# C of the first pair from unsplit float32 weights, by float32 products in two halves of the array

## The chip, the cores and the metric

One core of one Trainium2 chip runs the whole kernel. The metric is the device time of one execution in microseconds (us). Before the change it is 1462.33 us, the median of 3 runs (1460.45 to 1466.68).

## What is computed

The reference has three stages, in float32:

```python
p_packed = sm_attn(p, k, v)              # 8 batches, 8 heads, 576 keys, 32 packed rows, width 64
out = sm_attn(q, p_packed, p_packed)     # softmax attention of 576 queries over the 32 packed rows
x = out.transpose(0, 2, 1, 3).reshape(4608, 512)
g = x @ w_gate; val = x @ w_val          # 512 -> 1536
x = (g * sigmoid(g) * val) @ w_out       # 1536 -> 512
a = x @ w1; b = x @ w2                   # 512 -> 1024
out = ((a * b) @ w3) @ w_out2            # 1024 -> 1024 -> 512
```

The weights arrive as 8-byte floats and are turned into float32 on the chip by a few integer steps ("conversion" below).

## The kernel before, in words

**The front.** For each batch b and each half Q of its heads (16 units u), `p_packed` is formed, and `pa_PT` (line 544) puts its transpose into two tiles, `PTh` and `PTl`: a rounded high part (float32r) and the rest. The work of the front is placed by step numbers in a hand-written table (`task`, `run`); within it, the first weights are converted, split and stored as well.

**C instead of x @ w.** The gate and value products use that x is a softmax times `p_packed`: for a pair P of batches (4 pairs) and a slice f of 128 hidden columns (12 slices), `c_mm` (line 416) first forms C = p_packed transposed times the slice of `w_gate` and `w_val` (256 columns together), and `stage1` (line 643) multiplies the softmax weights by C. Exact float32 is kept by splitting: each factor is a high part and a low part, and three float32r products (high x high, high x low, low x high) take the place of one float32 product. So C costs 4 x 3 = 12 matmuls of 256 columns on the whole array (line 421), and the weights must be split beforehand by `w_split` (line 384): ACT copies the high part `wh`, POOL subtracts for the low part `wl`.

`c_out` (line 428) takes C out of PSUM and splits it in turn into `ch` (ACT, three copies) and `cl` (DVE, three subtractions). It takes three because the rows of the second batch stand in another order of the four blocks.

**The main loop** (line 857) goes over the 48 steps n = (P, f). In a step stand, in this order: `w_split` of step n+2, `wo_split`, `c_mm` of step n+1, `stage1` of the pair's first batch (`pg`, then `pv`: 12 matmuls of 288 columns each, line 655), the loads for later steps or, in pair 0, their conversion, half of `stage3` (`px`, 72 matmuls, line 680) where a group of three slices is complete, `stage1` of the second batch, parts of the query softmax of the next pair (`q_T`, `q_mm`; `psq`, line 207), and the other half of `stage3`. Each engine works through its own part in program order. In pair 0 (the first 12 steps) the conversions of all weights of `w_gate`, `w_val` and `w_out` are made as well: per step two of `wf` and one of `wof`, each three operations on DVE (lines 344, 351, 354) and one on ACT (line 341). Later pairs load the converted weights back from DRAM (`Wd`).

C of slices 0 and 1 of pair 0 is formed at the end of the front (steps 17.5 and 18.5 of the table), C of slices 2 to 11 in the main loop, in steps 1 to 10. C of all of pair 1 to 3 is formed in the main loop.

**Float32 products.** A few small products are made in plain float32 before the change too, in parts of the array: `q_mm` (line 198) has 8 calls with 32 weight columns each, which are placed at 4 column positions of the array. In the trace such a call stands as two instructions.

**PSUM.** Tiles of two banks go round: four in the main loop. The pool of the main loop is opened in step 0 and takes the banks of the front's pools; the first `pg` of the main loop takes those in which C of slice 1 stood.

Of the kernel before, what the change touches and what calls it, by code (L numbers as in the profile page):

```python
# [8 lines left out]
F32 = mybir.dt.float32  # L9
F32R = mybir.dt.float32r  # L10
# [13 lines left out]
SPD = 2.25  # L24
# [14 lines left out]
def packed_attention_moe_kernel(  # L39
# [24 lines left out]
    nc = tc.nc  # L64
# [13 lines left out]
    NPR = B // 2  # L78
# [4 lines left out]
    def pool(name, side, bufs=1, **kw):  # L83
        return tc.alloc_tile_pool(name=name, bufs=bufs, side=side, reuse_waits="tile", **kw)

    def sub(out, src, hi, on="dve"):
        eng = nc.vector if on == "dve" else nc.gpsimd
        eng.tensor_tensor(out=out, in0=src, in1=hi.bitcast(F32), op=ALU.subtract)  # L88
# [19 lines left out]
    wgv = pool("wgv", "right", bufs=2)  # L108
    pt_pool = pool("pt", "right")


    PTh = pt_pool.tile([128, 4, NPR, 128], F32R, name="PTh")
    PTl = pt_pool.tile([128, 4, NPR, 128], F32R, name="PTl")

    mask = const.tile([128, 2, 64], F32, name="mask")
    nc.vector.memset(mask, 0.0)
# [3 lines left out]
    vl = pool("vl", "left", bufs=2)  # L120
# [7 lines left out]
    def psum(name):  # L128
        ps_n[0] += 1
        return ps_at[ps_n[0] % len(ps_at)].tile([128, 2, 512], F32, tag="A", name=name)  # L130

    def psum1(name):
        return psB.tile([128, 512], F32, tag="B", name=name)
# [17 lines left out]
    def q_T(b, Q):  # L151
        t = q_t.pop((b, Q))
        qT = qp.tile([128, 2, S], F32, tag="qT", name=f"qT{b}_{Q}")
        for pr in range(2):
            nc.vector.transpose(out=qT[:, pr], in_=t[:, pr].rearrange("p n d -> p (n d)"))
        PT = qp.tile([128, 128], F32, tag="PT", name=f"PT{b}_{Q}")
        for e in range(2):
            cols = slice(64 * ((b + e) % 2), 64 * ((b + e) % 2) + 64)
            hi, lo = (x[:, 2 * Q + e, b // 2, cols].bitcast(F32) for x in (PTh, PTl))
            nc.vector.tensor_tensor(out=PT[:, 64 * e:64 * e + 64], in0=hi, in1=lo, op=ALU.add)  # L160
        qT_t[b, Q] = (qT, PT)

# [205 lines left out]
    W_t, wf_t, wst_t = {}, {}, {}  # L368

    def w_conv(f, gv):  # L370
        if gv == 0:
            wf_t[0, f] = wst_t[f] = vl.tile([128, 4, 2, 128], F32, tag="wf", name=f"wf0_{f}")
        t = wf_t[0, f]
        conv(f"w_{f}_{gv}", t[:, :, gv, :])

# [8 lines left out]
    def w_split(P, f):  # L384
        t = wf_t.pop((P, f))
        hi = wgv.tile([128, 4, 256], F32R, tag="wh", name=f"wh{P}_{f}")
        lo = wgv.tile([128, 4, 256], F32R, tag="wl", name=f"wl{P}_{f}")
        split(hi, lo, t.rearrange("p k g n -> p k (g n)"), sub_on="pool")
        W_t[P, f] = (hi, lo)
# [18 lines left out]
    C_t = {}  # L408

    def wo_split(P, f):  # L410
# [2 lines left out]
        split(hi, lo, wof_t.pop((P, f)), sub_on="pool")  # L413
        wo_t[P, f] = (hi, lo)

    def c_mm(P, f):
        wh, wl = W_t.pop((P, f))
        t = psum(f"pc{P}_{f}").rearrange("p a (k n) -> p (a k) n", k=2)
        for kt in range(4):
            for x, (a, w) in enumerate(((PTh, wh), (PTh, wl), (PTl, wh))):  # L420
                nc.tensor.matmul(t[:, kt], lhsT=a[:, kt, P, :], rhs=w[:, kt],  # L421
                                 start=(x == 0), stop=(x == 2))
        if C_t.get("later"):
            C_t["later"].append((P, f, t))
        else:
            c_out(P, f, t)

    def c_out(P, f, t):
        hi = cp.tile([128, 2, 2, 256], F32R, tag="ch", name=f"ch{P}_{f}")
        lo = cp.tile([128, 2, 2, 256], F32R, tag="cl", name=f"cl{P}_{f}")  # L430
        tv = t.rearrange("p (q e) n -> p e q n", e=2)
        nc.scalar.copy(hi[0:64], tv[0:64])
        for e in range(2):
            nc.scalar.copy(hi[64:128, 1 - e], tv[64:128, e])  # L434
        sub(lo[0:64], tv[0:64], hi[0:64])
        for e in range(2):
            sub(lo[64:128, 1 - e], tv[64:128, e], hi[64:128, 1 - e])
        C_t[P, f] = (hi, lo)
# [46 lines left out]
    def pa_s(u):  # L485


        kT = kT_t.pop(u)
        t = psum(f"psp{u}")
        for hq in range(4):  # L490
            for e in range(2):
                es = slice(64 * e, 64 * e + 64)
                nc.tensor.matmul(
                    t[hs[hq], e, 0:HS].rearrange("j (m p g) -> j g m p", m=3, g=3), lhsT=kT[es, 9, hs[hq]],
                    rhs=kT[es, 0:9, hs[hq]].rearrange("d (g m) p -> d g m p", g=3), start=True, stop=True, tile_position=(64 * e, 32 * hq))
        mx = pa.tile([128, 1], F32, tag="mx", name=f"mx{u}")
        nc.vector.reduce_max(mx, t[:, :, 0:HS], axis=AX.XY)
        nc.vector.tensor_scalar_mul(mx, mx, -scale)
        return t, mx
# [44 lines left out]
    def pa_PT(u):  # L544
        b, Q = divmod(u, 2)
        Pz = P_t.pop(u)
        tb = psum1(f"pPT{u}")
        t = tb[:, 0:128]
        nc.tensor.transpose(t, Pz.rearrange("p a b -> p (a b)"), ident)
        if u < 4:  # L550
            nc.tensor.transpose(tb[:, 128:256], Pd_t.pop(u).rearrange("p a b -> p (a b)"), ident)
            PTd = pa.tile([128, 128], F32, tag="PTd", name=f"PTd{u}", bufs=4)
            nc.scalar.copy(PTd, tb[:, 128:256])
            PTd_t[b, Q] = PTd
        at = [(2 * Q + e, b // 2, slice(64 * ((b + e) % 2), 64 * ((b + e) % 2) + 64)) for e in range(2)]
        for e in range(2):
            nc.scalar.copy(PTh[(slice(0, 128),) + at[e]], t[:, 64 * e:64 * e + 64])
        for e in range(2):
            sub(PTl[(slice(0, 128),) + at[e]], t[:, 64 * e:64 * e + 64], PTh[(slice(0, 128),) + at[e]])
# [12 lines left out]
    def task(s, fn, *args):  # L572
        extra.setdefault(s, []).append((fn, args))
# [8 lines left out]
    for s, (f, gv) in WS.items():  # L582
        task(s, w_conv, f, gv)
        for d in CVD:
            task(s + d, lambda: conv_rest.pop(0)())
        if gv == 1:
            task(s + STD, w_store, f)
            if f < 3:
                task(s + SPD, w_split, 0, f)
    task(WO0, wo_conv, 0)  # L590
    for d in CVD:
        task(WO0 + d, lambda: conv_rest.pop(0)())
# [12 lines left out]
    with tc.manual_schedule(engines=M0):  # L605
        for s in range(last + 1):
# [10 lines left out]
            if 0 <= s - 1 < U:  # L617
                x = pa_s(s - 1)
# [238 lines left out]
    for n, (P, f) in enumerate(steps):  # L857
        def at(i):
            return steps[n + i] if n + i < len(steps) else None

        if n > 0 and at(2) is not None:
            w_split(*at(2))
        wo_split(P, f)
        w3_task(P, f, 0)
        if n > 0 and at(1) is not None:
            c_mm(*at(1))
        if n == NPS:
            psC.release()
            psA.release()
            ps = tc.alloc_tile_pool(name="ps", bufs=4, space=bass.MemoryType.PSUM, reuse_waits="tile")  # L870
            ps_at[:] = [ps]
        stage1(2 * P, f)
        for what, nxt in (("w", at(3)), ("wo", at(1))):
            if nxt is not None:
                if nxt[0] > 0:
                    (w_load if what == "w" else wo_load)(*nxt)
                elif what == "w":
                    w_conv(nxt[1], 0)
                    w_conv(nxt[1], 1)
                    w_store(nxt[1])  # L880
                else:
                    wo_conv(nxt[1])
                    wo_store(nxt[1])
        w3_task(P, f, 1)
        if pend is not None:
            stage3(*pend, 0)
        w3_task(P, f, 2)
        stage1(2 * P + 1, f)
        i = n - NF
        if 0 <= i < len(w12_list):  # L890
            w12_conv(i)
        if P + 1 < NPR:
            q_tasks(2 * P + 2, 0, f)
            q_tasks(2 * P + 3, 5, f)
        if pend is not None:
            stage3(*pend, 1)
            pend = None
        C_t.pop((P, f))
        if f % GF == GF - 1:
            pend = (P, f // GF)  # L900
        if P == NPR - 1:
            if f == 0:
                aA.release()
                qp.release()
                wp = pool("wp", "left", bufs=2)
            w3_task(P, f, 3)
            if f == 9:
                assert w3_at[0] > len(w3_list)
                wp.release()
                vc.release()  # L910
                xp = pool("xp", "left", bufs=2)
                x2_prep(0, 0)
            if f == 10:
                x2_prep(0, 1)
                x2_prep(0, 2)
            if f == 11:
                x2_prep(0, 3)
                load_w12(0)
                ws_sums(0)
                for k in range(7):  # L920
                    ws_block(0, k)
# [169 lines left out]
```

## Time and profile before

| | |
|---|---|
| median of 3 runs | 1462.33 us |
| the profiled execution, its own time | 1462.87 us |
| its span (first to last instruction) | 1461.1 us |
| mean granted TensorE clock | 0.979 |
| PE busy | 95% of the span |
| DVE / ACT / POOL busy | 56% / 46% / 33% |

How to read it: PE is TensorE's matmuls, PEld its weight loads, DVE VectorE, ACT ScalarE, POOL GpSimd. "pc<-wh,PTh" means that the tile `pc` is written from the tiles `wh` and `PTh`. A share over the whole span mixes three stages: the front (to about 122 us), the main loop of 48 steps (to about 890 us), and a last stage of dense products. The change touches the front and the first quarter of the main loop only.

### The profile page before, as it was taken

The page shows a single profiled execution, that of the slowest core. Times are in us where ns is not written, and L with a number is a line of the kernel's source. Part 1 is how long each engine was busy: PE and PEld are TensorE (multiplying, and loading weights), DVE is VectorE, ACT ScalarE, POOL GpSimd, SP SyncE. Part 2 cuts the span into 40 slices and gives each one's busy share as a digit, 9 for nine tenths or more (in the row PEclk, how much of TensorE's full clock was granted, in tenths as well). Part 3 has the DMA queues.
Part 4 walks back from the last instruction along what each step waited for, and adds up shares of the span by engine and source line. Part 5 has one row for each costly group of instructions (what it writes and reads, how often), then busy time and mean ns, then how long its engine had stood idle before and what let it go on. Part 6 is the DMA issues. An engine that isn't in the chain of part 4 may idle for free.

```text
span 1461.1 us, 25415 instructions
## 1 busy us (share of the span) xinstructions
PE 1392.7 (95%) x9912; PEld 1308.5 (90%) x9912; DVE 816.9 (56%) x1220; ACT 667.0 (46%) x1117; POOL 486.4 (33%) x353
## 2 busy tenths in 40 slices
PE   6677989999999999999999999999999999999999
PEld 5467879998999999999999899989989999899997
DVE  3468899967877447566446737962333423334130
ACT  4576564546745356455553514643323323233231
POOL 0345344445443445435433312631202112021120
PEclk9788899999999999999999999999999999999999
DMA  9985565666553333114333324983736638366351
GB/s 277 245 225 174 145 174 161 187 198 184 140 163 72 108 90 82 52 51 166 109 132 121 123 68 142 322 291 118 255 111 203 194 123 252 108 208 189 126 170 44
DMA packets 175255, 230.25 MB, mean 158 GB/s; under 512 B 69408, under 2 KB 102176, under 8 KB 175136
## 3 DMA queue, kind: packets, MB, share of 16 engines
q1 hardware_dynamic: 175136, 228.64, 51.0%
q8 instruction: 78, 1.28, 0.3%
q14 instruction: 41, 0.34, 0.1%
HBM read 179.04 MB, written 49.55 MB: 156 GB/s over the span
## 4 chain that ended last, share of the span: by engine, by line
PE 72%; DVE 4%; ACT 2%; DMA 1%; issue 1%; POOL 0%; SPq 0%; DVEq 0%; ACTq 0%
PE px L680 15%; PE pA L964 14%; PE po L1028 13%; PE pB L964 7%; PE pg L655 6%; PE pv L655 6%; PE pC L964 3%; PE pc L421 3%; DVE cl L88 1%; DMA raw_w<-in_moe_w_dram 1%; DMA w12d<-w12t 1%; DVE u L662 1%; PE psq L207 1%; DVE acc L690 0%; DVE w12t L354 0%
## 5 line engine op out<-in xcount | busy, mean ns | idle before, releaser
L88 POOL TENSOR_TENSOR ul<-u,uh 128x576 fp32r<-128x576 f32 x96 | 145.5, 1520 | 224.2 <-ACT uh L92 224.1
L984 POOL TENSOR_TENSOR c<-s,s 128x384 f32<-128x384 f32 x48 | 48.8, 1017 | 376.7 <-ACT s L979 376.5
L680 PE MATMUL px<-uh,woh 128*128 128x288 f32 x768 | 166.1, 298 | 7.3 <-DVE cl L88 4.7
L680 PE MATMUL px<-ul,woh 128*128 128x288 f32 x768 | 165.4, 297 | 1.3 <-POOL ul L88 1.3
L680 PE MATMUL px<-uh,wol 128*128 128x288 f32 x768 | 165.5, 297 | 0.0
L88 POOL TENSOR_TENSOR wl<-wf,wh 128x1024 fp32r<-128x1024 f32 x48 | 117.8, 2453 | 135.0 <-ACT wh L92 115.4
L979 ACT COPY s<-pA 128x384 f32<-128x384 f32 x144 | 69.2, 481 | 181.7 <-PE pA L964 181.7
L88 DVE TENSOR_TENSOR cl<-pc,ch 64x1024 fp32r<-64x1024 f32 x144 | 120.6, 864 | 54.0 <-ACT ch L434 53.2
L680 PEld LDWEIGHTS px<-uh,woh 128*128 128x128 f32 x768 | 124.6, 190 | 9.8 <-DVE cl L88 5.1
L680 PEld LDWEIGHTS px<-ul,woh 128*128 128x128 f32 x768 | 124.4, 190 | 1.5 <-POOL ul L88 1.5
L680 PEld LDWEIGHTS px<-uh,wol 128*128 128x128 f32 x768 | 124.9, 190 | 0.0
L1028 PE MATMUL po<-wo_hi,abl 128*128 128x512 f32 x288 | 112.2, 389 | 0.0
L1028 PE MATMUL po<-wo_lo,abh 128*128 128x512 f32 x288 | 112.1, 389 | 0.0
L1028 PE MATMUL po<-wo_hi,abh 128*128 128x512 f32 x288 | 112.0, 389 | 0.0
L88 DVE TENSOR_TENSOR abl<-ab,abh 128x768 fp32r<-128x768 f32 x48 | 48.7, 1014 | 106.0 <-ACT abh L92 105.9
L92 ACT CAST uh<-u 128x576 fp32r<-128x576 f32 x96 | 64.7, 674 | 93.7 <-DVE u L662 93.4
L690 DVE TENSOR_TENSOR acc<-acc,px 128x576 f32<-128x576 f32 x96 | 70.9, 746 | 62.7 <-PE px L680 62.5
L662 DVE TENSOR_TENSOR u<-u,pv 128x576 f32<-128x576 f32 x96 | 72.1, 752 | 47.9 <-PE pv L655 42.5
L655 PE MATMUL pv<-aTh,ch 128*128 128x288 f32 x384 | 83.9, 300 | 7.8 <-ACT u L660 7.5
L88 POOL TENSOR_TENSOR wol<-wof,woh 128x512 fp32r<-128x512 f32 x48 | 65.5, 1378 | 74.6 <-ACT woh L92 65.9
L660 ACT ACTIVATE u<-pg 128x576 f32<-128x576 f32 x96 | 62.6, 652 | 60.6 <-PE pg L655 57.8
L655 PE MATMUL pg<-aTh,ch 128*128 128x288 f32 x384 | 83.9, 300 | 5.2 <-DVE cl L88 3.1
(358 smaller groups left out, 3627.2 us busy)
## 6 DMA issues: line engine op xcount, KB each, us to landing
ws<-wsd SPq DMA_DIRECT2D x245, 256.0 KB, 3.0
wf<-Wd SPq DMA_DIRECT2D x36, 512.0 KB, 3.4
raw_w<-in_moe_w_dram SPq DMA_DIRECT2D x32, 512.0 KB, 4.7
wsd<-ws SPq DMA_DIRECT2D x49, 256.0 KB, 3.0
raw_wo<-in_moe_w_out_dram SPq DMA_DIRECT2D x20, 512.0 KB, 4.2
km<-in_k_dram SPq DMA_DIRECT2D x16, 576.0 KB, 8.0
vm<-in_v_dram SPq DMA_DIRECT2D x16, 576.0 KB, 8.6
wof<-wod SPq DMA_DIRECT2D x36, 256.0 KB, 2.9
```

Source lines behind the costliest of these rows:

```text
L88: eng.tensor_tensor(out=out, in0=src, in1=hi.bitcast(F32), op=ALU.subtract)
L92: nc.scalar.copy(hi, src)
L421: nc.tensor.matmul(t[:, kt], lhsT=a[:, kt, P, :], rhs=w[:, kt], start=(x == 0), stop=(x == 2))
L655: nc.tensor.matmul(t[:, hf, 0:HS], lhsT=w[:, b % 2, Q, cols], rhs=x[:, Q, hf, :], start=first, stop=last,)
L660: nc.scalar.activation(u, t[:, :, 0:HS], AF.Silu)
L662: nc.vector.tensor_tensor(out=u, in0=u, in1=t[:, :, 0:HS], op=ALU.mult)
L680: nc.tensor.matmul(t[:, hf, 0:HS], lhsT=w[:, 128 * d:128 * d + 128], rhs=x[:, hf, :], start=first, stop=last,)
L690: nc.vector.tensor_tensor(out=o, in0=o, in1=t[:, :, 0:HS], op=ALU.add)
L964: nc.tensor.matmul(bk[n], lhsT=w[:, hl, 128 * d:128 * d + 128], rhs=r[:, d], start=(first and d == 0 and i == 0), stop=(d == 1 and i == 2) ...
L979: nc.scalar.copy(o, t)
L984: on.tensor_tensor(out=r, in0=o, in1=t, op=op)
L1028: nc.tensor.matmul(t, lhsT=a[:, j, cols], rhs=w[:, f], start=first, stop=last)
```

## The change

C of pair 0 is no longer formed from split factors. `pa_PT` writes the transposed `p_packed` of units 0 to 3 once, in float32, into a new tile `PT0`, and neither `PTh` nor `PTl` for them (these two lose their first pair). `c_first` forms C of pair 0 with 16 calls, each with all 128 rows, 64 weight columns and 256 moving columns in float32, alternately in the lower and the upper 64 columns of the array, and writes them already in the order that `stage1` wants. So `c_out` needs one copy and one subtraction for pair 0. `w_split` is not called for pair 0 any more, neither in the front (slices 0 to 2) nor in the loop. The converted weights of pair 0 stand in the buffers that held `wh` and `wl`, in turn, instead of those of `wf`.

```diff
+    PT0 = pt_pool.tile([128, 4, 2, 64], F32, name="PT0")
...
     def w_conv(f, gv):
         if gv == 0:
-            wf_t[0, f] = wst_t[f] = vl.tile([128, 4, 2, 128], F32, tag="wf", name=f"wf0_{f}")
+            wf_t[0, f] = wst_t[f] = wgv.tile([128, 4, 2, 128], F32, tag=("wh", "wl")[f % 2], name=f"wf0_{f}")
...
+    def c_first(f):
+        w = wf_t.pop((0, f))
+        t = psum(f"pc0_{f}").rearrange("p b (q n) -> p b q n", q=2)
+        for b in range(2):
+            for Q in range(2):
+                for e in (b, 1 - b):
+                    at = 64 * (e ^ b)
+                    nc.tensor.matmul(
+                        t[at:at + 64, b, Q], lhsT=PT0[:, 2 * Q + e, b],
+                        rhs=w[:, 2 * Q + e].rearrange("p g n -> p (g n)"),
+                        start=True, stop=True, tile_position=(0, at))
+        return t
+
     def c_mm(P, f):
+        if P == 0:
+            t = c_first(f)
+            if C_t.get("later"):
+                return C_t["later"].append((P, f, t))
+            return c_out(P, f, t)
...
     def c_out(P, f, t):
...
+        if P == 0:
+            nc.scalar.copy(hi, t)
+            sub(lo, t, hi)
+            C_t[P, f] = (hi, lo)
+            return
...
             PTd_t[b, Q] = PTd
+            nc.scalar.copy(PT0[:, 2 * Q:2 * Q + 2, b], t.rearrange("p (e j) -> p e j", e=2))
+            return
...
-            if f < 3:
-                task(s + SPD, w_split, 0, f)
...
-        if n > 0 and at(2) is not None:
+        if at(2) is not None and at(2)[0] > 0:
             w_split(*at(2))
```

## Rows read from the trace of the kernel before

**Rows 1.** The page, part 1: busy us, share of the span, instructions.

```profile
PE 1392.7 (95%) x9912; PEld 1308.5 (90%) x9912; DVE 816.9 (56%) x1220; ACT 667.0 (46%) x1117; POOL 486.4 (33%) x353
```

**Rows 2.** Stretches: length, busy PE, PEld, DVE, ACT, POOL; clock, DMA share, GB/s.

```profile
130.00:185.00 55.00, 50.30 (x360) 47.25 (x360) 49.12 (x57) 30.52 (x46) 23.49 (x14) 0.91 0.53 154
185.00:237.00 52.00, 44.39 (x326) 42.75 (x325) 51.74 (x66) 28.66 (x44) 22.18 (x13) 1.00 0.63 174
237.00:285.00 48.00, 45.60 (x357) 43.46 (x356) 45.34 (x65) 26.98 (x39) 20.88 (x12) 1.00 0.58 182
285.00:305.00 20.00, 18.89 (x143) 18.33 (x142) 18.98 (x25) 13.94 (x23) 13.04 (x8) 1.00 0.61 174
...
378.00:421.00 43.00, 43.00 (x328) 43.00 (x328) 36.24 (x45) 25.27 (x38) 22.02 (x13) 1.00 0.61 173
```

**Rows 3.** Waits of PE from 130 to 305 us: total, times, longest.

```profile
PE pv L655 <- ACT u L660: 5.7, 3, 2.8
PE px L680 <- DVE cl L88: 4.7, 2, 2.4
PE pc L421 <- DVE cl L88: 2.8, 4, 1.5
PE px L680 <- DVE sT L214: 1.9, 1, 1.9
PE pg L655 <- DVE u L662: 0.7, 1, 0.7
```

**Rows 4.** Groups by form, whole span: what splits C and the weights.

```profile
L88 POOL TENSOR_TENSOR wl<-wf,wh 128x1024 fp32r<-128x1024 f32 x48 | 117.8, 2453 | 135.0 <-ACT wh L92 115.4 <-issue 18.4 <-POOL ul L88 1.2
...
L88 DVE TENSOR_TENSOR cl<-pc,ch 64x512 fp32r<-64x512 f32 x96 | 62.5, 691 | 0.7
...
L88 DVE TENSOR_TENSOR cl<-pc,ch 64x1024 fp32r<-64x1024 f32 x48 | 58.2, 1212 | 53.3 <-ACT ch L434 53.2
...
L434 ACT CAST ch<-pc 64x512 fp32r<-64x512 f32 x96 | 51.3, 582 | 0.6
...
L92 ACT CAST wh<-wf 128x1024 fp32r<-128x1024 f32 x48 | 50.0, 1042 | 14.7 <-DVE wf L354 11.9 <-POOL wf L357 2.8
...
L432 ACT CAST ch<-pc 64x1024 fp32r<-64x1024 f32 x48 | 48.3, 1006 | 26.2 <-PE pc L421 26.2
```

**Rows 5.** A float32 product in four column positions: timeline, and its matmuls' durations (min/median/max).

```profile
173.97 0.43 PE L655 MATMUL pv<-aTh,cl 128*128 128x288 f32 x2
...
174.33 0.64 PEld L207 LDWEIGHTS psq<-qT,PT 128*32 128x32 f32 x16 [0.17 <-ACT wf L341]
174.33 1.18 PE L207 MATMUL psq<-qT,PT 128*32 128x288 f32 x16
...
175.81 0.42 PE L680 MATMUL px<-ul,woh 128*128 128x288 f32 x2
...
L207 PE MATMUL psq<-qT,PT x192: 406/406/689, 150.6 to 616.5; 128*32 128x288 f32 x192
```

**Rows 6.** C as it is now, timeline: its first of 12 matmuls, and what follows.

```profile
185.12 0.28 PE L421 MATMUL pc<-wh,PTh 128*128 128x256 f32 x1
...
186.56 0.42 PE L655 MATMUL pg<-aTh,ch 128*128 128x288 f32 x2
```

**Rows 7.** DVE beside POOL, timeline.

```profile
142.02 2.40 POOL L88 TENSOR_TENSOR wl<-wf,wh 128x1024 fp32r<-128x1024 f32 x1 [1.71 <-ACT wh L92]
142.05 2.91 DVE L354 SCALAR_TENSOR_TENSOR wof<-raw_wo,vx_wo 128x512 int32<-128x512 int32 x1
...
258.26 0.68 DVE L354 SCALAR_TENSOR_TENSOR wof<-raw_wo,vx_wo 128x512 int32<-128x512 int32 x1
```

**Rows 8.** The end of the front: a stretch (columns as in rows 2), and timeline.

```profile
107.00:122.00 15.00, 8.54 (x130) 7.61 (x130) 9.93 (x23) 12.09 (x25) 8.01 (x6) 0.73 0.53 154
...
119.24 2.52 DVE L88 TENSOR_TENSOR cl<-pc,ch 64x1024 fp32r<-64x1024 f32 x3
121.91 0.82 PE L655 MATMUL pg<-aTh,ch 128*128 128x288 f32 x2 [3.10 <-DVE cl L88]
```

More of the change, by code (lines that the diff above doesn't have):

```diff
@@ L109, in packed_attention_moe_kernel @@
     pt_pool = pool("pt", "right")
-    PTh = pt_pool.tile([128, 4, NPR, 128], F32R, name="PTh")
-    PTl = pt_pool.tile([128, 4, NPR, 128], F32R, name="PTl")
+    PTh = pt_pool.tile([128, 4, NPR - 1, 128], F32R, name="PTh")
+    PTl = pt_pool.tile([128, 4, NPR - 1, 128], F32R, name="PTl")
+    PT0 = pt_pool.tile([128, 4, 2, 64], F32, name="PT0")
     mask = const.tile([128, 2, 64], F32, name="mask")
@@ L158, in q_T @@
             cols = slice(64 * ((b + e) % 2), 64 * ((b + e) % 2) + 64)
-            hi, lo = (x[:, 2 * Q + e, b // 2, cols].bitcast(F32) for x in (PTh, PTl))
+            hi, lo = (x[:, 2 * Q + e, b // 2 - 1, cols].bitcast(F32) for x in (PTh, PTl))
             nc.vector.tensor_tensor(out=PT[:, 64 * e:64 * e + 64], in0=hi, in1=lo, op=ALU.add)
@@ L420, in c_mm @@
             for x, (a, w) in enumerate(((PTh, wh), (PTh, wl), (PTl, wh))):
-                nc.tensor.matmul(t[:, kt], lhsT=a[:, kt, P, :], rhs=w[:, kt],
+                nc.tensor.matmul(t[:, kt], lhsT=a[:, kt, P - 1, :], rhs=w[:, kt],
                                  start=(x == 0), stop=(x == 2))
[L423 to L426, printed above, removed]
+        c_out(P, f, t)
     def c_out(P, f, t):
@@ L554, in pa_PT @@
             PTd_t[b, Q] = PTd
-        at = [(2 * Q + e, b // 2, slice(64 * ((b + e) % 2), 64 * ((b + e) % 2) + 64)) for e in range(2)]
+            nc.scalar.copy(PT0[:, 2 * Q:2 * Q + 2, b], t.rearrange("p (e j) -> p e j", e=2))
+            return
+        at = [(2 * Q + e, b // 2 - 1, slice(64 * ((b + e) % 2), 64 * ((b + e) % 2) + 64)) for e in range(2)]
         for e in range(2):
```

## The prediction, made blind

> **What bounds the kernel now.** I read the page's busy times first: PE is busy 95% of the span [rows 1], so at first sight every microsecond added to PE is paid and none taken from another engine is won. That holds for the mean, not for the stretch that changes, so I cut the loop into stretches of three steps [rows 2]. In pair 1, from 378 to 421 us, PE is busy all 43 us while DVE has 36. In pair 0 the reader should see the two change places: from 185 to 237 us DVE is busy 51.7 of 52 us and PE only 44.4. From 130 to 305 us PE's busy times add to 159.2 of 175 us, so it stands still for 15.8. The waits of PE there give the same 15.8 us (5.7 + 4.7 + 2.8 + 1.9 + 0.7) and name who is late: ACT's `u`, and DVE's `cl`, `sT` and `u` [rows 3]. In the first stretch the granted clock is 0.91 [rows 2]: 0.09 / 0.5 x 55 = 10 us at the lower level, 1.2 GHz, where PE had just stood still. Up to 2 of these lie in the waits themselves, and half of the other 8, so 4 us, is lost work. So pair 0 holds about 19.8 us (15.8 + 4) that a PE with everything ready would not need. This is all that the loop can give back.
>
> **Part 1: the products of C.** Now C is 12 matmuls, 185.12 to 186.56: 1.44 us [rows 6]. The new form is not in the trace. The nearest is `psq`: float32, all 128 rows, in column parts of the array, with 8 calls that stand as 16 instructions [rows 5]. They take 1.18 us from the first start to the last end, and each lasts 0.406 us. Were they one after the other, 16 streams would not fit, so four run side by side, in four rounds: (1.18 - 0.406) / 3 = 0.258 us per round of 288 columns. For 256 columns that is 0.229. Twice the present pitch (1.44 / 12 = 0.12 per 256 columns of float32r) would be 0.24, so a float32 instruction streams at about half the pace of a float32r one. The new C has 16 calls, 32 instructions; in two halves that is 16 rounds, 3.5 to 3.7 us. Entering and leaving the parts of the array costs too. From 173.97 to 175.81 lie the block and two pairs of ordinary matmuls, one ahead of it and one behind [rows 5]. At the pace of rows 6 a pair takes 2 x 0.12 x 288 / 256 = 0.27 us, so the block has 1.84 - 0.54 = 1.30, and less 4 x 0.25 of streaming 0.3 us are left [rows 5, 6]. I take 3.5 + 0.25 = 3.75 us, 2.3 us more than now. Ends: 3.45 without any switch (+2.0), and 16 x 0.229 + 0.31 = 3.97 (+2.5). Ten C's stand in the main loop, where nothing hides PE's work: +22.5 us (20 to 25).
>
> **Part 2: what leaves DVE, ACT and POOL in pair 0.** Per step [rows 4]: three subtractions of `cl` (1.21 + 2 x 0.69 = 2.59 us) become one over as many elements per partition as the first of them, about 1.21, so DVE loses 1.4. ACT loses two of the three copies (2 x 0.58) and `wh` (1.04): 2.2 us. POOL loses `wl`, 2.45 us. POOL's loss is DVE's gain as well: an operation of DVE that takes 0.68 us by itself took 2.91 while `wl` ran, and ended after it [rows 7]. Over the nine C's from 130 to 285 us DVE has 146.2 us of 155 [rows 2]; less 9 x 1.4 it has 134, and if half of the time of nine `wl` was DVE standing still (9 x 2.45 / 2 = 11), 123. PE has 140.3 + 9 x 2.3 = 161. So DVE would be at 76 to 83% of PE, where pair 1 has 84% and no idle PE [rows 2]. I therefore let PE become the bound again, and most of the waits go: 14 of the 15.8 us, and the 4 us of clock with the stall before it. Late next is ACT's `u`, the longest wait now [rows 3], and what the `wl` of pair 1 hold up, which POOL still makes in the last two steps. Ends: 4 us and 19.8.
>
> **Part 3: the front.** Two C's stand there, at a mean clock of 0.73 [rows 8]; they take 2.3 us more each at the full clock and 4.6 at the lower one. The main loop begins when `cl` of the second has released its PSUM banks: 119.24 + 2.52 = 121.76, `pg` at 121.91 after 3.10 us of waiting [rows 8]. Ahead of that go three `wh` (3.1 us of ACT), three `wl` (7.4 us of POOL), two thirds of `ch` and half of `cl` for two slices (DVE 2.8 us, ACT 2.3). The longer C's delay the last units' products on PE by about as much, as these queue behind them. I take -1.5 us; ends -6 (the 2.8 of DVE, one `wh`, and 2 us of clock after a busier PE) and +5 (both C's at the lower clock, 9.2, less the relief of some 4). The single copy into `PT0` instead of two copies and two subtractions for four units is off the path: these units are done long before the last.
>
> **Part 4: buffers and DMA.** The converted weights go to the four buffers of `wh` and `wl`. The conversion for step n+3 takes the buffer of slice n-1, whose C was formed in step n-2, and whose store was issued in step n-4, so neither is late; pair 1's first split takes buffers read in step 7. Same stores and loads on SP, in the same order: no cost. If that cover failed, a conversion would wait for a store to land; `c_first` comes two steps later, and a step of pair 0 lasts 17 us now (155 us for nine), so PE would see only a delay beyond that.
>
> **The sum.** 22.5 - 14 - 4 - 1.5 = +3.0 us. The profiled execution took 1462.87 us, 0.5 above the median of the runs, so I forecast 1465.5 us. A measurement of this kernel can tell about 0.5%, 7.3 us, from no change: that is 1455 to 1469.6.
>
> **Rivals.**
>
> *The stalls stay* (slower). DVE's queue in pair 0 remains the place where the step is set, because POOL's `ul` and `wol` stop DVE as `wl` did, and a longer PE step only moves the waits. For it: DVE was full for 52 us [rows 2]. Against: pair 1 runs at 84% with the same `ul`, `wol` and even `wl`. It decides from the point where less than 22.5 - 1.5 - 7.3 = 13.7 of the 19.8 us come back. With 4 coming back and nothing from the front it is 22.5 - 4 = +18.5: 1481 us. Chance 0.20.
>
> *The front and all stalls give back* (faster). 20 us for the C's, less 19.8, less 6 in the front: -6, or 1457 us; below 1455 only if the clock of the first loop steps rises as well. Chance 0.12.
>
> *The halves take turns.* If two parts of 64 columns don't run side by side, there are 32 rounds: 32 x 0.22 + 0.25 = 7.3 us, +5.9 each, +59 in the loop, less 19.8, and some +8 in the front: 1509 us. Against it stand four parts side by side in `psq`; for it, that no row shows 64 columns. Chance 0.06.
>
> *Weight loads don't hide.* In `psq` the 16 weight loads end 0.64 us after the first start, half a microsecond before the last matmul does, so they ran under the matmuls [rows 5]. If a round instead waited for its load, at 0.15 us each (between 0.64 / 16 = 0.04 and a whole round's 0.258 [rows 5], for want of a nearer row the middle), C would take 16 x 0.15 = 2.4 us more, +24 in ten steps: all stalls returned, 22.5 + 24 - 19.8 = +27, 1489 us. The Trainium skill (TensorE: Matmul & The Clock Gate, Part 3) says that loads overlap matmuls in flight only where the groups of rows differ; here every part uses all rows, so by that rule this rival would come true, and the trace of `psq`, also all rows, disagrees. Chance 0.04.
>
> **How the numbers follow.** The forecast's own case has 0.58, by its ends 1459 to 1472. A range that leaves out the halves taking turns, the dearest of the weight-load case and the outer tails of the first two rivals is 1457 to 1484. Faster by over 0.5%: half of the second rival and a trace of the forecast, 0.08. Slower: most of the first rival (0.17), the last two (0.10) and the upper end of the forecast (0.09): 0.36. Within: 0.56.
>
> **What would show it.** `pc` of pair 0 as 32 instructions in rounds of about 0.22 us, 3.75 us in all; DVE under 85% from 130 to 290 us; PE's waits there under 5 us in total; the clock at 1.00 from 130 us on; the first `pg` of the loop within 119 to 123 us; `c12`'s place, and all after it, later by 3 us or so. I am wrong if a C takes 5 us or more, if PE's waits in pair 0 stay over 10 us, or if the loop starts over 5 us from where it did.

## The result, and the profile after

The changed kernel takes 1443.53 us (median; 1441.93 to 1444.94), the kernel before 1463.14 us on the same chip (1460.45 to 1466.68). The ratio is 0.9858, with a 95% interval of 0.9839 to 0.9876. So the change wins 20 us, where the prediction had a loss of 3: the forecast, its range and its likeliest sign were all wrong. The execution profiled here took 1441.93 us (span 1440.2), against 1462.87 before.

One number in the text ahead is false. "The change" and Part 1 say that `c_first` has 16 calls. Its three loops, over b, Q and e, have two turns each: 2 x 2 x 2 = **8 calls**, or 16 instructions, half of what the forecast paid for.

First the page's busy times (columns as in [rows 1]):

```profile
PE 1393.1 (97%) x9960; PEld 1302.1 (90%) x9960; DVE 780.2 (54%) x1188; ACT 642.5 (45%) x1077; POOL 457.7 (32%) x341
```

PE's busy time is what it was (1392.7), while the span is 21 us shorter. PE does not do less; it stands still less. DVE is busy 37 us less, ACT 24.5, POOL 29. The stretches of [rows 2] show where; after:

```profile
130.00:185.00 55.00, 55.00 (x431) 49.53 (x430) 43.44 (x65) 31.09 (x47) 15.75 (x11) 1.00 0.62 176
185.00:237.00 52.00, 52.00 (x400) 48.22 (x399) 44.58 (x62) 23.79 (x37) 17.92 (x13) 1.00 0.67 195
237.00:285.00 48.00, 47.97 (x369) 45.05 (x369) 42.01 (x58) 25.81 (x37) 21.52 (x13) 1.00 0.64 170
```

PE is busy all the time, so these stretches hold more work than they did. For the same work, from the first C of the main loop to the tenth (nine C's), before and after:

```profile
130.35:285.42 155.07, 140.37 (x1038) 133.53 (x1037) 146.62 (x186) 86.41 (x127) 66.20 (x38) 0.97 0.58 169
```

```profile
127.35:265.92 138.57, 138.57 (x1073) 126.68 (x1072) 119.23 (x171) 71.37 (x103) 44.50 (x30) 1.00 0.67 189
```

PE was busy 140.4 of 155.1 us and now all of 138.6, and the granted clock went from 0.97 to 1.00. DVE fell from 146.6 to 119.2 us. The waits of PE from 119 to 310 us, where [rows 3] had five lines and 15.8 us:

```profile
PE pg L676 <- DVE cl L88: 1.4, 1, 1.4
```

That one wait is the loop's start, which was 3.1 us [rows 8]. In the main loop of pair 0 not one wait is left. What C costs PE now, in the timeline of a step in the same place as [rows 6]:

```profile
174.02 0.42 PE L701 MATMUL px<-uh,wol 128*128 128x288 f32 x2
174.37 1.95 PE L424 MATMUL pc<-wf,PT 128*64 128x256 f32 x16
176.25 0.54 PE L676 MATMUL pg<-aTh,ch 128*128 128x288 f32 x2
176.62 0.42 PE L676 MATMUL pg<-aTl,ch 128*128 128x288 f32 x2
```

From the last pair of `px` to the second pair of `pg` are 2.60 us; two ordinary pairs take 0.54, so C holds PE for **2.06 us**, 0.62 more than the 1.44 of [rows 6]. The list of the tile's instructions (count, then shortest, median and longest in ns) says how it streams:

```profile
L424 PEld LDWEIGHTS pc<-wf,PT x192: 132/137/232, 106.8 to 267.3; 128*64 128x64 f32 x192
L424 PE MATMUL pc<-wf,PT x192: 379/379/690, 106.8 to 267.5; 128*64 128x256 f32 x192
```

192 instructions for 12 C's are 16 each. The first start and the last end of a C lie 1.95 us apart; less the 0.379 of one matmul, 1.57 us for seven steps make eight rounds of two, 0.224 us apart.

On DVE, three groups from 130 to 285 us, before (busy us, mean ns):

```profile
L354 DVE SCALAR_TENSOR_TENSOR wof<-raw_wo,vx_wo 128x512 int32<-128x512 int32 x10 | 13.3, 1328 | 0.1
L88 DVE TENSOR_TENSOR cl<-pc,ch 64x512 fp32r<-64x512 f32 x18 | 11.7, 691 | 0.1
L88 DVE TENSOR_TENSOR cl<-pc,ch 64x1024 fp32r<-64x1024 f32 x9 | 10.8, 1205 | 0.9 <-ACT ch L434 0.9
...
L160 DVE TENSOR_TENSOR PT<-PTh,PTl 128x64 f32<-128x64 f32 x8 | 6.0, 769 | 0.0
```

and after:

```profile
L88 DVE TENSOR_TENSOR cl<-pc,ch 128x1024 fp32r<-128x1024 f32 x10 | 12.1, 1211 | 3.6 <-ACT ch L448 3.6
L355 DVE SCALAR_TENSOR_TENSOR wof<-raw_wo,vx_wo 128x512 int32<-128x512 int32 x10 | 8.0, 804 | 0.0
...
L161 DVE TENSOR_TENSOR PT<-PTh,PTl 128x64 f32<-128x64 f32 x8 | 1.6, 210 | 0.0
```

The subtractions of C are one pass instead of three (22.5 us for nine C's become 12.1 for ten, 10.9 for nine). So of the 27.4 us that DVE lost over the same work they are 11.6. The other two groups were not changed at all: the last step of the ten conversions of `wof` takes 0.80 us each instead of 1.33, the eight sums for `PT` 0.21 instead of 0.77, 9.7 us together. Most of the other 15.8 us was DVE standing still inside its own instructions; single groups vary from run to run, so the tests below are read by DVE's total over nine C's.

**Where the 20.9 us lie.** The first `pg` of the loop starts 2.5 us earlier (119.42 against 121.91). The second C of pair 1 is the next mark, before:

```profile
302.75 0.39 PE L421 MATMUL pc<-wh,PTh 128*128 128x256 f32 x1 [0.27 <-DVE cl L88]
```

and after:

```profile
282.42 0.39 PE L440 MATMUL pc<-wh,PTh 128*128 128x256 f32 x1
```

That is 20.3 us earlier: 17.8 were won in the loop of pair 0, although ten C's cost 6.2 more there. The stretches between the two marks, before and after:

```profile
121.91:302.75 180.84, 165.03 (x1204) 157.63 (x1205) 171.06 (x220) 103.28 (x152) 81.91 (x47) 0.96 0.59 171
```

```profile
119.42:282.42 163.00, 162.97 (x1245) 149.82 (x1245) 138.01 (x196) 85.67 (x124) 60.53 (x39) 0.99 0.67 188
```

Behind the mark the lead dips and comes back, 0.6 us more in all. From 305 to 700 us the profiled execution has one wait (3.3 us, below), the kernel before four, of 3.4 us in all. A second profiled execution of the changed kernel took 161.69 us from mark to mark, and had three waits behind it, of some 7 us in all.

### The profile page after: what moved, and what is told of

It is laid out like the page before. It is cut to its first block, busy times and chain, and to the rows that moved or that the text cites. A ratio compares the mean times of both kernels' runs of the same rounds, so it can differ in the third digit from the quotient of the medians.

```text
span 1440.2 us, 25384 instructions
## 1 busy us (share of the span) xinstructions
PE 1393.1 (97%) x9960; PEld 1302.1 (90%) x9960; DVE 780.2 (54%) x1188; ACT 642.5 (45%) x1077; POOL 457.7 (32%) x341
## 5 line engine op out<-in xcount | busy, mean ns | idle before, releaser
L88 DVE TENSOR_TENSOR cl<-pc,ch 64x512 fp32r<-64x512 f32 (+2 forms) x120 | 105.1, 900 | 55.4 <-ACT ch L455 47.6
L88 POOL TENSOR_TENSOR wl<-wf,wh 128x1024 fp32r<-128x1024 f32 x36 | 86.9, 2414 | 97.4 <-ACT wh L92 86.7
L676 PE MATMUL pg<-aTl,ch 128*128 128x288 f32 x384 | 83.3, 299 | 0.0
```

Of the source, the lines that this page charges most:

```text
L676: nc.tensor.matmul(t[:, hf, 0:HS], lhsT=w[:, b % 2, Q, cols], rhs=x[:, Q, hf, :], start=first, stop=last,)
```

## The experiments

Four theories stood. **The count**: the forecast's method held, and the eight calls that it counted too many are most of its miss. Of what freed DVE, three more: **A**, either relief would have done alone, and only both loads together bring waits back; **B**, what counts is the split of the weights on ACT and POOL; **C**, what counts is DVE's own subtractions of C. In the tests below, but for e5, the changed kernel is the base, and one thing is put back or changed; "back" is what a run is slower than its 1443.53 us.

**e1: the calls that were counted.** Each of the eight products is issued twice, so that there are 16 calls.

```diff
-                for e in (b, 1 - b):
+                for e in (b, 1 - b, b, 1 - b):
```

> The changed kernel, with each of the 8 float32 products of a C of pair 0 issued twice (the second writes the same values over the first): 16 products per C, the number that the prediction counted. Theory (PE is the bound of pair 0 after the change, and the miss is the count): a C takes 8 rounds of 0.216 us more, 3.7 instead of 2.0 us, all of it paid in the ten C's of the loop: 17 us more than the changed kernel's 1443.5, and 2 to 5 us more in the front at the lower clock: 1461 to 1466 us, where the prediction stood. Rival (DVE and ACT still set the pace of pair 0, and PE has slack there): less than 9 us more, under 1452 us, and PE's waits shrink instead.

Measured: 1465.87 us (1464.85 to 1469.26), ratio to before 1.0021 (1.0002 to 1.0040). Its timeline:

```profile
181.22 0.42 PE L701 MATMUL px<-uh,wol 128*128 128x288 f32 x2
181.58 3.67 PE L424 MATMUL pc<-wf,PT 128*64 128x256 f32 x32
185.18 0.54 PE L676 MATMUL pg<-aTh,ch 128*128 128x288 f32 x2
185.56 0.42 PE L676 MATMUL pg<-aTl,ch 128*128 128x288 f32 x2
```

By the same reading C holds PE for 4.34 - 0.54 = 3.80 us, against the 3.75 of the forecast, and the kernel takes the 1465.5 us that were forecast. The kernel that was priced blind is this one. That the two agree to 0.4 us has some luck in it: ten C's cost 23.6 us more than before, where 22.5 were forecast, and as the kernel before took 1463.69 beside it, all the rest gave back 21.4, where 19.5 were forecast. The eight extra rounds cost 3.80 - 2.06 = 1.74 us, or 0.217 each, and ten C's 17.4 of the 22.3 us between the two kernels; the front is 1.9 us later, and 2.2 us of waits stand in the loop again.

**e2: C's three copies and three subtractions back.** The products stay as changed.

```diff
-            nc.scalar.copy(hi, t)
-            sub(lo, t, hi)
+            nc.scalar.copy(hi[0:64], t[0:64])
+            for e in range(2):
+                nc.scalar.copy(hi[64:128, e], t[64:128, e])
+            sub(lo[0:64], t[0:64], hi[0:64])
+            for e in range(2):
+                sub(lo[64:128, e], t[64:128, e], hi[64:128, e])
```

> The changed kernel, with C of pair 0 taken out of PSUM in three copies and three subtractions again, as before. DVE gets 1.4 us more per C, ACT 1.2. Theory A (DVE's queue overflowed only by the sum of its own subtractions and its stops beside POOL, so that either alone fits under PE): 1 to 5 us more than the changed kernel's 1443.5, 1444 to 1449 us, with PE's waits from 119 to 285 us under 5 us. Theory B (POOL's low parts made all the stalls): no more than 1 us. Theory C (the subtractions made them): over 10 us, 1454 us or more.

Measured: 1457.99 us, ratio 0.9957 (0.9940 to 0.9975): 14.5 us back. The profiled execution is the longest of the six (1461.20). Its stretch of nine C's:

```profile
128.56:275.96 147.40, 140.20 (x1074) 126.73 (x1073) 136.06 (x189) 81.53 (x123) 44.80 (x30) 1.00 0.62 184
```

DVE is at 136.1 us, 16.8 more than in the changed kernel, though POOL has no `wl` to make for pair 0 (44.8 us, against 44.5). The two passes more per C are 11.7 of that. So here DVE is late mostly by its own work.

**e3_idle_split: the split of the weights back.** In steps 1 to 9 ACT's copy and POOL's subtraction are made as before, into buffers that nobody reads.

```diff
+    def w_idle(f):
+        hi = vl.tile([128, 4, 2, 128], F32R, tag="wf", name=f"ih{f}")
+        lo = vl.tile([128, 4, 2, 128], F32R, tag="wf", name=f"il{f}")
+        split(hi, lo, wf_t[0, f], sub_on="pool")
...
+        elif n > 0 and at(2) is not None:
+            w_idle(at(2)[1])
```

> The changed kernel, which in the loop's steps 1 to 9 also makes the split of the weights of pair 0 (ACT's copy of the high part, POOL's subtraction of the low part, at the place where it stood before), into buffers that nobody reads. Theory A (either alone fits under PE): 1 to 5 us more, 1444 to 1449 us. Theory B (POOL's low parts made the stalls): 10 us or more, from 1453 us, with single operations of DVE of 2 us and more beside POOL's and PE's waits over 10 us in pair 0. Theory C (the subtractions of C made them): no more than 1 us.

Measured: 1458.19 us, ratio 0.9942 (0.9910 to 0.9974): 14.7 back, with DVE's subtractions still in one pass. Four of its five executions lie between 1458.13 and 1459.44, one took 1447.59. DVE has 132.1 us over nine C's, 12.9 more than in the changed kernel, though no instruction was added on DVE.

**e3_idle_three: both.** The edits of the last two together.

> Both at once: the idle split of the weights of pair 0 in the loop, and C of pair 0 taken out in three copies and three subtractions. What is left of the change in the loop is the products themselves and the buffers. Theory A (the sum of both overfills DVE's queue): over 12 us more than the changed kernel's 1443.5, 1456 us or more, and more than the two single runs add up to. Theories B and C: no more than the larger of the two single runs and 2 us. If the loop's gain lay in the new buffers for the converted weights, or in the products, all three runs stay within 3 us of 1443.5.

Measured: 1463.23 us, ratio 0.9993 (0.9979 to 1.0008): 19.7 back, the time of before. The largest of its waits of PE from 117 to 305 us:

```profile
PE pc L429 <- DVE cl L88: 4.1, 3, 2.4
PE pg L685 <- DVE cl L88: 2.7, 1, 2.7
PE px L710 <- DVE cl L88: 2.0, 2, 1.1
PE px L710 <- DVE sT L215: 2.0, 1, 2.0
```

DVE has 144.5 us over nine C's. A fell twice: each load alone brings back more than two thirds of the gain, and the two together bring 19.7, less than the 29.2 of their sum. B and C each named a half. Both loads lie on the same queue, DVE's, and once it is late, more work on it costs less than the first did. The ten C's still cost 6.2 us more than before here, yet the time is that of before: beside a late DVE the longer C takes the place of waits (13.8 us in the loop, against 15.8) and of time at the lower clock, while in the changed kernel all that e1 adds is paid.

**e3_idle_pool and e3_idle_act: which half of the split.** Only POOL's subtraction, or only ACT's copy, is put back, against the changed kernel and in the same steps. POOL has no high part to read here, so it subtracts the weights from themselves. The expectations call it D that POOL alone does it, through DVE, and E that ACT's queue does.

```diff
+    def w_idle(f):
+        lo = vl.tile([128, 4, 2, 128], F32R, tag="wf", name=f"il{f}")
+        w = wf_t[0, f]
+        nc.gpsimd.tensor_tensor(out=lo, in0=w, in1=w, op=ALU.subtract)
```

```diff
+    def w_idle(f):
+        hi = vl.tile([128, 4, 2, 128], F32R, tag="wf", name=f"ih{f}")
+        nc.scalar.copy(hi, wf_t[0, f])
```

> The changed kernel with only POOL's part of the idle split: one subtraction of 1024 elements per partition in each of the loop's steps 1 to 9, into a buffer that nobody reads. Theory D (pair 0 now runs just under the edge of DVE's queue, and DVE stops while POOL subtracts, so this alone pushes it over): 8 to 14 us more than the changed kernel's 1443.5, 1451 to 1458 us, with the idle split of both engines at 1458. Theory E (it was ACT: its copy of the high part waits for the converted weights and holds up the activation behind it): under 4 us more.

> The changed kernel with only ACT's part of the idle split: one copy of 1024 elements per partition in each of the loop's steps 1 to 9, into a buffer that nobody reads. Theory E (ACT's copy waits for the converted weights and holds up the activation behind it): 8 to 14 us more than 1443.5, with PE's waits on ACT's u. Theory D (DVE beside POOL): under 4 us more.

Measured: POOL alone 1452.67 us, ratio 0.9925 (0.9902 to 0.9947), 9.1 back; ACT alone 1443.01 us, ratio 0.9870 (0.9840 to 0.9899), nothing back that its interval of some 4 us either way can show; its profiled execution has one wait of 2.2 us. How POOL does it, in the timeline of its run:

```profile
204.61 1.89 POOL L388 TENSOR_TENSOR il<-wf 128x1024 fp32r<-128x1024 f32 x1 [3.36 <-DVE wf L355]
...
205.06 1.73 DVE L345 TENSOR_SCALAR vx_wo<-raw_wo 128x512 int32<-128x512 int32 x1
```

A step of the conversion that DVE makes in 0.41 us at its shortest in this trace takes 1.73 beside POOL's subtraction and ends after it. The stretches of nine C's say the same, with POOL's subtraction and with ACT's copy:

```profile
125.45:269.86 144.41, 140.06 (x1073) 126.89 (x1072) 127.95 (x169) 70.83 (x103) 60.58 (x39) 1.00 0.64 181
```

```profile
121.93:264.32 142.39, 140.22 (x1074) 128.22 (x1073) 120.14 (x171) 79.90 (x114) 45.11 (x31) 0.99 0.66 187
```

With one instruction per step added on POOL and none on DVE, DVE has 128.0 us, 8.7 more than the 119.2 of the changed kernel; with ACT's copy it has 120.1. The Trainium skill (SBUF — State Buffer, "SBUF: two separate sides") says that DVE and GpSimd share a pair of ports by an exclusive lock, which the one that starts first holds for its whole instruction: of DVE one in a two-port mode or, against a GpSimd instruction that reads SBUF, one with two inputs in SBUF. The conversion's last step has two such inputs, and [rows 7] agree: its 2.91 us start 0.03 us behind POOL's 2.40 and end behind them. Which mode the step with one input was in, no run here shows.

ACT's copy and POOL's subtraction together cost 14.7 us where the one costs 9.1 and the other nothing, but the two tests do not add up to the third. POOL's subtraction takes 1.95 us by itself and 2.77 in the run with both, 15.6 against 22.1 us for eight; DVE stands still for 8.7 against 12.9 us, 0.56 and 0.58 for each microsecond of POOL's. So most of the difference is the length of the subtraction. What ACT adds beyond that stays open; in the run with both, the largest wait is for ACT's `u` (4.6 us), which in the run with ACT's copy alone is 2.2.

**e5: one pass of copies and subtractions in the kernel before.** The split products stay. The blocks of the second batch then stand in the wrong order: that part of the computation is changed.

```diff
+        if P == 0:
+            nc.scalar.copy(hi, t.rearrange("p (b q) n -> p b q n", b=2))
+            sub(lo, t.rearrange("p (b q) n -> p b q n", b=2), hi)
+            C_t[P, f] = (hi, lo)
+            return
```

> The kernel before, with its split products and splits of the weights, but C of pair 0 taken out in one copy and one subtraction; the blocks of the second batch then stand in another order, so this part of the result is another one. What is left of the old form beside the changed kernel: C 0.6 us shorter on PE, and the split of the weights. Theory (DVE's queue fills from two sides, and either side alone brings back most of the waits): the idle split cost 14.7 us on top of the changed kernel; with C 6 us shorter that makes 1450 to 1457 us. Rival (the new buffers or the unsplit weights matter in another way): outside 1446 to 1460.

Measured: 1455.22 us, ratio 0.9934 (0.9912 to 0.9956), against 1465.0 for the kernel before on the same chip: 9.8 us for this part alone, half of the gain, without any float32 product. DVE has 129.1 us over nine C's, against 146.6 before.

**e4: unsplit float32 on the whole array.** Four calls of 128 columns per C; C then comes in the old order, and takes three copies and subtractions as before. `PT0` is filled by two copies per unit for it.

```diff
+        t = psum(f"pc0_{f}").rearrange("p a (k n) -> p (a k) n", k=2)
+        for kt in range(4):
+            nc.tensor.matmul(t[:, kt], lhsT=PT0[:, kt, :],
+                             rhs=w[:, kt].rearrange("p g n -> p (g n)"),
+                             start=True, stop=True)
```

> The changed kernel with C of pair 0 from unsplit float32 products on the whole array: 4 products with 128 weight columns in place of 8 with 64, so C comes in the old order of blocks and needs three copies and three subtractions. No change of the array's parts: C 1.75 us instead of 2.05, 3 us less in ten steps than the run with three pieces and the halves (1458): 1453 to 1458 us. If the halves brought more than the order of the blocks (a float32 product of 128 columns streams slower than two of 64 side by side), C takes 3 us or more and the time is above 1462. If the halves are what costs, it is under 1448.

Measured: 1448.72 us, ratio 0.9904 (0.9880 to 0.9929): 5.2 back, better than expected. Its timeline:

```profile
187.15 0.43 PE L669 MATMUL pv<-aTh,cl 128*128 128x288 f32 x2
187.41 1.89 PE L421 MATMUL pc<-wf,PT 128*128 128x256 f32 x8
188.95 0.62 PE L669 MATMUL pg<-aTh,ch 128*128 128x288 f32 x2
189.41 0.43 PE L669 MATMUL pg<-aTl,ch 128*128 128x288 f32 x2
```

C holds PE for 2.26 - 0.54 = 1.72 us: eight instructions with no change of array parts, 0.34 less than in halves. So the halves cost 0.34 per C on PE, and what they buy is the order of the rows that makes one pass of copies possible. Against e2, which shares its DVE work, this kernel is 9.3 us faster. Ten C's of 0.34 are 3.4 of that; its waits in pair 0 are 8.4 us instead of 9.3, and e2's profiled execution has one more of 2.2 us near 400 us. For the remaining 2.8 the clock is at hand: from 290 to 410 us the granted clock is 0.97 in e2 and 1.00 here, 3.6 us of work at the most. That is one execution of each.

**e6: unsplit float32 halves in all four pairs.** `c_first` takes the pair as an argument, and no weight of the gate and value products is split any more. The later pairs' weights are loaded into the buffers of `wh` and `wl` too, and a copy takes the place of the sums for `PT`.

```diff
-                        t[at:at + 64, b, Q], lhsT=PT0[:, 2 * Q + e, b],
+                        t[at:at + 64, b, Q], lhsT=PT0[:, 2 * Q + e, 2 * P + b],
...
-        if at(2) is not None and at(2)[0] > 0:
-            w_split(*at(2))
```

> The unsplit products in two halves for C of all four pairs: no split of these weights anywhere, one copy and one subtraction per C everywhere, and the query products read the unsplit tile. Theory (outside pair 0 PE is the bound and the relief of the other engines is worth nothing): 36 C's at 2.05 in place of 1.44 us, 22 us more, less up to 5 us of waits in the first steps of pair 1: 1460 to 1466 us. Rival (the relief counts in all pairs): under 1450 us.

Measured: 1466.11 us, ratio 1.0016 (0.9999 to 1.0033): 22.6 slower than the change alone. In the stretch of pair 1 that [rows 2] show:

```profile
378.00:421.00 43.00, 43.00 (x334) 39.38 (x333) 21.72 (x31) 13.34 (x21) 12.37 (x9) 1.00 0.40 125
```

DVE falls to 21.7 us of 43, and nothing comes of it: PE was full there before (43.00) and is full now. At 0.62 us each, 36 more C's are 22.3 us, all of them paid. The same edit wins 20 us where DVE is the bound and loses 22 where PE is.

**e7: the wait that is left.** The changed kernel's wait at 314 us, on ACT and DVE:

```profile
312.50 0.66 ACT L342 ACTIVATE w12t<-raw_w 128x512 f32<-128x512 f32 x1 [5.79 <-DMA w12d<-w12t]
313.20 0.69 DVE L352 SCALAR_TENSOR_TENSOR vx_w<-w12t,vx_w 128x512 int32<-128x512 int32 x1 [2.40 <-ACT w12t L342]
313.92 1.65 DVE L355 SCALAR_TENSOR_TENSOR w12t<-raw_w,vx_w 128x512 int32<-128x512 int32 x1
315.60 1.38 DVE L345 TENSOR_SCALAR vx_w<-raw_w 128x512 int32<-128x512 int32 x1
316.90 0.74 DVE L711 TENSOR_TENSOR acc<-acc,px 128x576 f32<-128x576 f32 x1
```

and on PE:

```profile
317.70 0.85 PE L676 MATMUL pg<-aTh,ch 128*128 128x288 f32 x2 [3.35 <-DVE acc L711]
318.34 0.68 PE L676 MATMUL pg<-aTl,ch 128*128 128x288 f32 x2
```

DVE's sum `acc`, for which PE waits, stands behind a conversion of the later stages' weights (`w12t`) that itself waits for ACT, and ACT waits for the store of an earlier block (`w12d<-w12t`). Behind the wait PE's pairs follow each other every 0.48 us instead of every 0.27, and the granted clock from 314 to 323 us is 0.67, where it was 1.00 from 300 to 314. Two mends: these conversions three steps later, or three buffers in place of two for them (and for the other tiles that share these buffers).

```diff
-        i = n - NF
+        i = n - NF - 3
```

```diff
-        t = vl.tile([128, 512], F32, tag="vu", name=f"w12t{i}")
+        t = vl.tile([128, 512], F32, tag="vu", name=f"w12t{i}", bufs=3)
```

> The changed kernel, with the conversion of the weights of the last stage three steps later (steps 15 to 30 in place of 12 to 27), so that it does not fall in with the end of pair 0. After the change the loop has one wait of PE of 3.3 us behind DVE's sum for px at 314 us, with a lower clock behind it; ACT there waits for the store of a converted block. Theory (the gain of pair 0 is partly given back there): 2 to 5 us less than the changed kernel, 1438 to 1442 us. Rival (the wait moves on with the conversions): within 1 us of it.

> The changed kernel, with three buffers in place of two for these converted blocks, so that a conversion does not wait for the store of the block two before it. Theory: the wait of PE at 314 us goes, 2 to 5 us less than the changed kernel, 1438 to 1442 us. Rival (the store is not what is late, the loads are): within 1 us of it.

> The changed kernel itself, beside the runs of this call: 1443.5 us, within 2.

Measured, on one chip: the changed kernel again 1442.65 us, ratio 0.9843 (0.9824 to 0.9861); later conversions 1445.40, ratio 0.9864 (0.9849 to 0.9880); three buffers 1441.94, ratio 0.9835 (0.9814 to 0.9856). Neither wins: the first is 2.8 us slower than the changed kernel beside it, with none of its four executions among the other's, and the second is within 1 us, as its rival had it. With later conversions the wait for `acc` is 2.0 us; with three buffers the one at 314 us is gone, and others stand up, of up to 2.0 us. Single waits vary: `px` waits for `cl` for 2.1 us near 387 us in the first, and as long in the second execution of the changed kernel. No version that ran clearly beats the changed kernel.

## Why the prediction was wrong, step by step

**Part 1, the products of C: the step that failed.** "The new C has 16 calls, 32 instructions": it has 8 and 16. The method held. Rounds of 0.229 us per 256 columns (from `psq`) or 0.24 (twice the float32r pace) were read, 0.22 was used, and 0.217 is measured; 0.3 us were put on the change of array parts, and 2.06 - 8 x 0.217 is 0.32. With the right count the forecast's own terms give 8 x 0.22 + 0.25 = 2.0 us, +0.6 per C and +6 for ten instead of +22.5, a sum of 6 - 14 - 4 - 1.5 = -13.5, and 1449 us. So the miscount is 16.5 of the 22 us by which the forecast missed, and e1, which has the calls that were counted, takes the time that was forecast. The diff gave the number: three loops of two turns each. The trace gave a second one, since C has 4 blocks of weight rows by 2 batches, eight products of 64 columns without the split.

**Part 2, what leaves DVE.** Right in kind and too timid. For nine C's DVE was to have 123 to 134 us, and has 119.2: it lost 27.4 us, where 12.6 to 23.6 were forecast. The subtractions are 11.6 of that, against 12.6, and the rest, most of it standing still, 15.8, against 0 to 11. DVE is at 86% of PE's 138.6 us, above the 76 to 83% that were forecast for a longer PE and near the 84% that pair 1 lives with [rows 2]. From that "14 of the 15.8 us" of waits were to go; all went. That DVE gains through POOL as well, taken from [rows 7] at half of each `wl`, is confirmed by the run with POOL's subtraction alone, which gives 9 us back. ACT's relief, named beside them, shows no gain by itself.

**A wait costs more than its idle time.** In the loop 17.8 us were won. Waits of 15.8, 4 of clock, less 6.2 for C are 13.6, so 4.2 are missing from the forecast's terms even with C and the waits as measured. The clock is 1.8 of them: at the lower level, half the speed, half of the time is lost work, so a stretch loses its length times what its mean clock lacks to 1.00. With the mean clocks above, 0.96 and 0.99 (0.959 and 0.991 with a digit more), that is 7.3 us of the 180.84 before and 1.5 of the 163.00 after, 5.8 less (some tenths of it lie in the waits), where the forecast took 4, from the stretch from 130 to 185 us alone. Most of the other 2.4 stands in the trace of before, at the 1.9 us wait of [rows 3]:

```profile
157.58 0.42 PE L655 MATMUL pv<-aTh,cl 128*128 128x288 f32 x2
159.85 0.50 PE L680 MATMUL px<-uh,woh 128*128 128x288 f32 x2 [1.85 <-DVE sT L214]
160.19 0.45 PE L680 MATMUL px<-ul,woh 128*128 128x288 f32 x2
```

The two pairs are 2.27 us apart where 0.27 would do, so 2.00 are lost and 1.85 shown: the idle time is counted from the drawn end of a matmul, which lies behind the place where the next could have started. The first pair after the wait takes 0.34 until the next instead of 0.27. That is 0.2 us for each of the 11 waits, some 2.4 in all, by this one wait; it is read from rows, not tested. The runs with something put back, each in its profiled execution, from the first `pg` to the second C of pair 1 (163.00 us in the changed kernel):

| kernel | longer by, us | PE's waits there, us | more lost to the clock, us | left, us | medians: back, us |
|---|---|---|---|---|---|
| the change, with ACT's copy | 2.4 | 2.2 | 0.2 | 0.0 | 0 |
| with POOL's subtraction | 6.4 | 4.5 | 0.0 | 1.9 | 9.1 |
| with C's three passes (e2) | 12.5 | 9.3 | 2.0 | 1.2 | 14.5 |
| with the split of the weights | 14.2 | 9.4 | 3.4 | 1.4 | 14.7 |
| with both | 17.6 | 13.8 | 1.9 | 1.9 | 19.7 |

So waits and clock together are most of what the loads cost, and 1.2 to 1.9 us are left where several waits stand, roughly 0.2 each. By the medians, the loads that cost anything cost 1.4 to 2 us for each microsecond of wait that the profile shows. Each row is one execution, and loop starts differ by some 5 us between these runs, so single rows are rough.

**Part 3, the front.** The forecast was -1.5 us, with `pg` between 119 and 123; it came at 119.42, -2.5. The two C's there were overpriced by the same count. The place varies: in a second execution of the changed kernel `pg` came at 117.83, and the kernel before has one trace.

**Part 4, buffers and DMA.** From 119 to 310 us PE waits for no store and no weight buffer, and no engine for a store of `wf`, as forecast. ACT does wait there for stores of other weights (`w12t`), 15.4 us in all (7.0 before, from 119 to 330 us), and the wait of PE at 314 us that comes of them was not foreseen.

**The rivals.** *The stalls stay* was refuted: no wait is left. *The front and all stalls give back* has its mechanism confirmed, but by the false count it ended at 1457 us, and so the way that it went was given 0.08. *The halves take turns* is refuted by eight rounds, not sixteen, for 16 instructions (sixteen of 0.217 us would be 3.5 us, and a C takes 2.06). *Weight loads don't hide* is refuted too: the loads last 0.137 us, and rounds follow each other every 0.217, so nothing is left between two rounds in which two of them could stand. By one of its rules the Trainium skill (TensorE: Matmul & The Clock Gate, Part 3) lets a load overlap running matmuls only where the groups of rows differ; here every product uses all 128 rows, and the trace disagrees with that rule.

## What to carry to other kernels

Count added work by multiplying the ranges of its loops, and set the product beside a second count from the mathematics; a factor of two in the one term with a sign against the change turns the verdict round. Before pricing an engine's relief, find the stretch where another engine waits for it: the same edit won 20 us where DVE was the bound (pair 0) and lost 22 where PE was (pairs 1 to 3). Loads on a nearly full queue don't add up, so test a cause by putting back one at a time, and the pair as well.

## What the runs showed of the hardware that was not expected

- Instructions of DVE that a change doesn't touch can get much shorter when POOL's subtraction beside them is gone: `PT`'s sums went from 0.77 to 0.21 us. With nine subtractions put back on POOL alone DVE is busy 8.7 us longer over nine C's and the kernel is 9.1 us slower. DVE's busy time counts this standing still as work. The mean of one group can mislead: the last step of the `wof` conversions went from 1.33 to 0.80 us, but is at 1.14 in the run with ACT's copy, which has no such subtraction.
- Unsplit float32 costs PE little in this place: 1.72 us on the whole array against 1.44 for three split float32r products of the same C, and it needs no split weights at all.
- The two halves of the array add 0.34 us per C to that. At the 0.215 us per instruction of the whole array (1.72 / 8), a block of 8 rounds has 0.34 left and one of 16 rounds (e1) 0.36, so this goes with the block, the way in and out, and not with the rounds.
